# Maxima over partitions of kept attention chunks by VectorE's 32x32 block transposes in place of TensorE's transposes, two more chunks computed twice, and a lower limit on VectorE's shifts

## The chip, the cores and the metric

The kernel runs on one core of one Trainium2 chip. The metric is the device time of one execution in microseconds (us); lower is better. A core has five engines that run side by side, each with its own in-order queue: PE (TensorE, matrix products and transposes), ACT (ScalarE), DVE (VectorE), POOL (GpSimd) and SP (SyncE, which issues all DMAs here). In the profile, PEld is TensorE's load of the stationary operand, which overlaps PE. PE writes to PSUM only; POOL cannot read PSUM. [...]

## The reference, cut to what matters

Two independent layers share the launch, and their outputs are joined along the last axis:

```python
# A: Fourier mixing, S = 2048, D = 448
a = einsum("bsd,ed->bse", x, dft_hid_re);  b = einsum("bsd,ed->bse", x, dft_hid_im)
y = einsum("ts,bse->bte", dft_seq_re, a) - einsum("ts,bse->bte", dft_seq_im, b)
# B: attention, H = 16 heads of Dh = 28
q, k, v = split(x @ wqkv)
p = softmax(einsum("bhqd,bhkd->bhqk", q, k) * Dh**-0.5)
o = concat_heads(einsum("bhqk,bhkd->bhqd", p, v)) @ wo
out = concatenate([y, o], axis=-1)
```

The softmax subtracts each row's maximum over all 2048 keys. The change touches how that maximum is found and applied, for part of the rows.

## The kernel before, in words

**Precision and tiles.** Matrix products run on 32-bit operands split in a high and a low part (three products stand for one). `P = 128`, `CH = 512`, `NT = 16` key tiles, `NC = 4` query chunks of 512 queries for each head. A unit is one (head, chunk) pair; there are 64 of them. Scores are computed transposed, keys on partitions and 512 queries along the free axis, so the maximum over keys goes over 16 tiles and over the 128 partitions of each.

**Two kinds of units.** `TWICE` lists for each head which chunks are computed twice; all others are kept.

- `unit_twice` (lines 743 to 789; 16 units before the change): 16 score products with the queries on partitions (L754), each reduced by DVE along the free axis (L758), one reduction of the 16 results (L762), a small PE transpose (L717), a split in high and low part (L766 on ACT, L767 on DVE), a store of the two rows to DRAM (L770) and their load into two extra rows of the query tile (L771). Then 16 score products again (L782), now with the maximum already subtracted by the extra rows, and 16 exponentials of 512 (L786 on ACT).
- `unit_kept` (lines 791 to 853; 48 units before): 16 score products (L804), each copied from PSUM to SBUF pairs (`kept`, copies at L415, ACT for the most part, DVE for some at L417) and folded by DVE into a running maximum `rm` of 128 x 512 (first L811, then L814). Then the maximum over the 128 partitions: four PE transposes of 128x128 (`turn`, L821), a DVE reduction to 128x4 with the sign changed (L823), four PE transposes of a broadcast operand (`spread`, L830) that leave the negated maximum of each query in all 128 partitions of a PSUM bank `pm`, and an ACT copy of it to `mb` in SBUF (L832). Then each of eight pairs (128x1024) is shifted by it: on POOL with `mb`, or on DVE with `pm` (both L847; DVE may take pairs `i < DVE_SHIFT`, and any pair near the end, `LATE`), and exponentiated on ACT (L851).

Both end in products with the values (`pv_group`, L735) and a copy of the result (`unit_out`); `out_of` (L866 to L884) folds, normalises and stores; the output projection (L976) comes last, with operands split at L958 and L411.

**The fill.** The projections (`project`, `values`), the Fourier layer's first product (`hidden`; all at L547) and its second (`sequence`, L662) are PE work that needs few other engines: weights are loaded (L515), copied to a high part on ACT (L516), and the low part is taken on POOL (L522).

**What sets the order.** Nothing is ordered by hand. `Schedule` (lines 170 to 314) is a planner that runs while the program is built: every task has an engine (or a choice of engines), an assumed cost, a key (a due time) and slots of buffers; it simulates the engines and hands each free engine the ready task with the lowest key, and the program's order on every engine is that. The costs at lines 389 and 390 are its assumptions (`DVE_P = 0.60` for a DVE operation of 512). Kept and twice units form two lanes, with due times spread evenly from `T_ATT` to `T_END` (lines 420 to 429); the fill's keys are spread by `fkey`. At run time the engines meet only through semaphores, and the order does not adapt.

**Buffers at the change.** `rm`, `mb` and `n2` have one slot each, `nm` three; six of eight PSUM banks serve attention (`bank_s`), two the fill.

Of the kernel before, what the change touches and what calls it, by code (L numbers as in the profile page):

```python
# [11 lines left out]
F32 = mybir.dt.float32  # L12
# [10 lines left out]
H = 16  # L23
DH = 28
P = 128
# [5 lines left out]
SCALE = DH ** -0.5  # L31

NKEPT = 19
DVE_SHIFT = 4
LATE = 110.0
NKEYS = 8
NFILL = 2
# [1 line left out]
N_WARM = 11  # L39
GV = 8  # L40

TWICE = [(1,) for h in range(H - 2)] + [(3,), (3,)]
OUT_DVE = True

LAST = (0, 1, 3, 2)
# [2 lines left out]
def f32(ap):  # L48
    return ap.bitcast(F32)
# [268 lines left out]
def tile_kernel(ctx, tc, xa, wre, wim, wd, xb, wqkv, wo, out):  # L318
# [8 lines left out]
    def new(name, shape, dtype=F32, n=None, in_turn=False):  # L327
        if n is None:
            return sb.tile(shape, dtype, tag=name, name=name)
        sch.pools.append(Slots([sb.tile(shape, dtype, tag=f"{name}{i}", name=f"{name}{i}") for i in range(n)], in_turn))  # L330
        return sch.pools[-1]
# [25 lines left out]
    sm_s = new("sm", [P, NT], F32, 1)  # L357
    mx_s = new("mx", [P, 4, NC], F32, 1)
    nm_s = new("nm", [P, 4], F32, 3)
    n2_s = new("n2", [4, 2, P], F32R, 1)  # L360
    banks = [ps.tile([P, CH], F32, tag=f"bank{i}", name=f"bank{i}") for i in range(8)]

    w_first = Weights(lent, held=True)
# [23 lines left out]


    M512, M448, MS = 0.2335, 0.2065, 0.2365
    ACT_P, ACT_S, DVE_P, POOL_2 = 0.48, 0.52, 0.60, 1.25  # L390

    def pe(key, emit, n=1, d=MS, lat=0.25, **kw):
        return sch.add({"PE": n * d}, key, emit, lat=lat, **kw)
# [5 lines left out]
    def act(key, emit, d=ACT_P, **kw):  # L399
        return sch.add({"ACT": d}, key, lambda e: emit(), **kw)  # L400

    def dve(key, emit, d=DVE_P, **kw):
        return sch.add({"DVE": d}, key, lambda e: emit(), **kw)
# [20 lines left out]
    P_R = (T_END - T_ATT) / (len(lane_r) + 1.5)  # L424
    P_K = (T_END - T_ATT) / (len(lane_k) + 1.5)
    due = {}
    for lane, per, ahead, part in ((lane_r, P_R, 1.08, 1.0), (lane_k, P_K, 1.8, 1.0)):
        for i, u in enumerate(lane):
            due[u] = (T_ATT + i * per, T_ATT + (i + ahead) * per, part * per / 16)
    head_due = [min(due[h, c][0] for c in range(NC)) for h in range(H)]  # L430
# [312 lines left out]
    def unit_twice(u):  # L743
        h, c = u
        t_a, t_b, dt = due[u]
        q = q_s.slot()
        lq = load_q(u, q)
        mx, nm = mx_s.slot(), nm_s.slot()
        ms = []
        for kc in range(NC):  # L750
            for qt in range(4):
                o = bank_s.slot()
                key = t_a + (kc * 4 + qt) * dt
                m = pe(key, lambda e, o=o, kc=kc, qt=qt: nc.tensor.matmul(  # L754
                    o.t, q.t[:KR, qt * P:(qt + 1) * P], KT[h][kc].t[:KR, :], start=True, stop=True),
                    deps=[*lq, *got_k[h, kc], before.get("ra")], use=[o, q, KT[h][kc], mx])
                in_line("ra", m)
                ms.append(dve(key - 20, lambda o=o, kc=kc, qt=qt: nc.vector.tensor_reduce(  # L758
                    mx.t[:, qt, kc:kc + 1], o.t, axis=AX.X, op=ALU.max), deps=[m],
                    use=[o, mx]))  # L760
        key = t_a + 16 * dt - 20
        r = dve(key, lambda: nc.vector.tensor_reduce(nm.t, mx.t, axis=AX.X, op=ALU.max, negate=True), 0.2,  # L762
                deps=ms, acq=[nm], use=[mx])
        o, n2 = bank_s.slot(), n2_s.slot()
        t = max_rows(key, o, nm, r)
        a = act(key, lambda o=o: nc.scalar.activation(n2.t[:, 0, :], o.t[:4, :P], AF.Copy), 0.2, deps=[t], acq=[n2], use=[o])  # L766
        b = dve(key, lambda o=o: nc.vector.tensor_tensor(n2.t[:, 1, :], o.t[:4, :P], f32(n2.t[:, 0, :]), op=ALU.subtract), 0.25,  # L767
                deps=[a], use=[o, n2])
        nd = nm_d[h * NC + c]
        s = dma(key, lambda: nc.sync.dma_start(nd.rearrange("r (a b) -> a r b", a=4), f32(n2.t)), size=4, deps=[b], use=[n2])  # L770
        ld = dma(key, lambda: nc.sync.dma_start(f32(q.t)[KR:KR + 2, :], nd), size=4, deps=[s], use=[q])  # L771
        po = bank_s.slot()
        last_pv = None
        for g in range(NT // GV):
            tiles, es = [], []
            for kt in range(GV * g, GV * (g + 1)):
                o = bank_s.slot()
                if kt % 2 == 0:
                    tiles.append(kept_s.slot())
                p = Half(tiles[-1], kt % 2)  # L780
                key = t_b + kt * dt
                m = pe(key, lambda e, o=o, kt=kt: nc.tensor.matmul(  # L782
                    o.t, KT[h][kt // 4].t[:KR + 2, kt % 4 * P:(kt % 4 + 1) * P], q.t[:KR + 2, :], start=True, stop=True),
                    deps=[ld, before.get("rb")], use=[o, p.pair, q, KT[h][kt // 4], po])
                in_line("rb", m)
                es.append(act(key - 20, lambda o=o, p=p: nc.scalar.activation(p.t, o.t, AF.Exp, scale=SCALE),  # L786
                              deps=[m], use=[o, p.pair]))
            last_pv = pv_group(u, g, tiles, [*es, last_pv], po, key)
        unit_out(u, po, last_pv, key - 20)

    def unit_kept(u):
        h, c = u
        t_a, t_b, dt = due[u]
        q = q_s.slot()
        lq = load_q(u, q)
        rm, nm, mb = rm_s.slot(), nm_s.slot(), mb_s.slot()
        kept, cs = [], []
        for kt in range(NT):
            o = bank_s.slot()
            if kt % 2 == 0:  # L800
                kept.append(kept_s.slot())
            s = Half(kept[-1], kt % 2)
            key = t_a + kt * dt
            m = pe(key, lambda e, o=o, kt=kt: nc.tensor.matmul(  # L804
                o.t, KT[h][kt // 4].t[:KR, kt % 4 * P:(kt % 4 + 1) * P], q.t[:KR, :], start=True, stop=True),
                deps=[*lq, *got_k[h, kt // 4], before.get("ka")], use=[o, s.pair, rm, q, KT[h][kt // 4]])
            in_line("ka", m)
            cs.append(sch.add({"ACT": ACT_P, "DVE": DVE_P} if kt == 1 else {"ACT": ACT_P}, key - 20,
                              lambda e, o=o, s=s: copy_of(e, s.t, o.t), deps=[m], use=[o, s.pair], lock=[o]))
            if kt == 1:  # L810
                prev = dve(key - 20, lambda o=o, s=kept[0]: nc.vector.tensor_tensor(rm.t, o.t, s.t[:, 0, :], op=ALU.max),  # L811
                           deps=[m, cs[0]], use=[rm, o, kept[0]], lock=[o], own=RAW)
            elif kt:
                prev = dve(key - 20, lambda o=o: nc.vector.tensor_tensor(rm.t, o.t, rm.t, op=ALU.max),  # L814
                           deps=[m, prev], use=[rm, o], lock=[o], own=RAW)
        key = t_a + 16 * dt - 20
        o = bank_s.slot()

        def turn(e, o=o):
            for i in range(4):  # L820
                nc.tensor.transpose(o.t[:, i * P:(i + 1) * P], rm.t[:, i * P:(i + 1) * P], ident)  # L821
        t = pe(key, turn, d=0.45, deps=[prev], use=[o, rm])
        r = dve(key, lambda o=o: nc.vector.tensor_reduce(  # L823
            nm.t, o.t.rearrange("p (a b) -> p a b", a=4), axis=AX.X, op=ALU.max, negate=True), deps=[t], use=[o, nm])

        pm = bank_s.slot()

        def spread(e):
            for i in range(4):
                nc.tensor.transpose(pm.t[:, i * P:(i + 1) * P], nm.t[:, i:i + 1].to_broadcast([P, P]), ident)  # L830
        t = pe(key, spread, d=0.45, deps=[r], use=[pm, nm])
        ld = act(key, lambda: nc.scalar.activation(mb.t, pm.t, AF.Copy), deps=[t], use=[pm, mb], lock=[pm])  # L832
        po = bank_s.slot()
        last_pv = None
        pairs = NT // 2

        def over_pair(t):
            return bass.AP(tensor=t.tensor, offset=t.offset, ap=[t.ap[0], [0, 2], [1, CH]])

        for g in range(NT // GV):  # L840
            es = []
            for i in range(GV // 2 * g, GV // 2 * (g + 1)):
                s = kept[i]
                key = t_b + 2 * i * dt

                def shift(e, s=s):
                    eng[e].tensor_tensor(s.t, s.t, over_pair(pm.t if e == "DVE" else mb.t), op=ALU.add)  # L847
                on_dve = i < DVE_SHIFT or due[u][0] > T_END - LATE
                sh = sch.add({"POOL": 2.36, "DVE": 1.13} if on_dve else {"POOL": 2.36}, key, shift,
                             deps=[ld, t, cs[2 * i], cs[2 * i + 1]], use=[s, mb, *([pm] if on_dve else [])])  # L850
                es.append(act(key, lambda s=s: nc.scalar.activation(s.t, s.t, AF.Exp, scale=SCALE), 0.96, deps=[sh], use=[s]))  # L851
            last_pv = pv_group(u, g, kept[GV // 2 * g:GV // 2 * (g + 1)], [*es, last_pv], po, key)
        unit_out(u, po, last_pv, key - 20)
# [168 lines left out]
```

## Time and profile before

| what | value |
|---|---|
| median of three runs | 1169.23 us (1166.75 to 1170.17) |
| the profiled execution's own time | 1167.41 us |
| its span from first to last instruction | 1165.6 us |
| mean granted TensorE clock | 0.998 |
| instructions | 19879 |
| DVE reductions at L823, one for each kept unit | 48 |
| DVE reductions at L762, one for each twice unit | 16 |

Busy time is the union of an engine's instructions; an instruction's mean duration can be longer than its turn on the engine, because the next one starts while it ends. In the lists of groups the columns are: line, engine, operation, operands (output, then inputs), shapes, count, then busy us and mean ns of one, then idle time of the engine ahead of them and what ended it. A timeline row begins with start and length in us from the span's start.

### The profile page before, as it was taken

The numbers are of one execution on the slowest core, as the hardware profiler recorded it, in microseconds if no ns is written. First come the engines' busy times: TensorE is split into PE (matmuls) and PEld (weight loads), VectorE is DVE, ScalarE is ACT, GpSimd is POOL, SyncE is SP. The second block draws the span as 40 slices with busy tenths as digits, with TensorE's granted clock in tenths as the row PEclk, the third lists the DMA queues.
The fourth block names the chain that finished last, engine by engine and source line by source line (L and its number), as shares of the span: only waits on it lengthen the run. The fifth ranks groups of instructions, "written<-read, shape, count | busy, mean of one in ns | idle before, by whom it ended". The sixth has DMA issues, their size and how long they took to land.

```text
span 1165.6 us, 19879 instructions
## 1 busy us (share of the span) xinstructions
PE 1155.8 (99%) x6426; PEld 810.0 (69%) x6426; DVE 934.8 (80%) x1473; ACT 1054.0 (90%) x1773; POOL 908.1 (78%) x530
## 2 busy tenths in 40 slices
PE   8999999999999999999999999999999999999998
PEld 7876666676766766766766676767767666667687
DVE  6699978888878878887888889888888878878742
ACT  5279999999999999999999999999999999999942
POOL 2167768999888889888978998998887898996830
PEclk9999999999999999999999999999999999999999
DMA  8892345231323242322223332323224333223552
GB/s 257 178 212 105 120 126 179 75 92 58 95 79 105 70 117 70 99 78 90 87 89 91 94 113 71 99 74 107 90 80 117 90 102 94 86 70 88 181 166 105
DMA packets 111736, 125.18 MB, mean 107 GB/s; under 512 B 49264, under 2 KB 63216, under 8 KB 111632
## 3 DMA queue, kind: packets, MB, share of 16 engines
q1 hardware_dynamic: 111632, 123.91, 36.0%
q8 instruction: 51, 0.84, 0.3%
q14 instruction: 53, 0.43, 0.1%
HBM read 89.98 MB, written 33.75 MB: 106 GB/s over the span
## 4 chain that ended last, share of the span: by engine, by line
PE 94%; DVE 2%; POOL 1%; issue 1%; ACT 1%; DMA 1%; SPq 0%; DVEq 0%; ACTq 0%
PE bank L662 27%; PE bank L735 19%; PE bank L804 15%; PE bank L547 13%; PE bank L782 5%; PE bank L754 5%; PE bank L976 3%; PE bank L821 2%; PE bank L830 2%; PE bank L866 1%; DVE rm L814 1%; POOL kept L847 1%; DMA kept<-wqkv 0%; DVE big L411 0%; ACT kept L415 0%
## 5 line engine op out<-in xcount | busy, mean ns | idle before, releaser
L847 POOL TENSOR_TENSOR kept<-kept,mb 128x1024 f32<-128x1024 f32 x262 | 626.0, 2412 | 111.1 <-ACT mb L832 87.3
L814 DVE TENSOR_TENSOR rm<-bank,rm 128x512 f32<-128x512 f32 x672 | 460.4, 685 | 74.9 <-ACT kept L415 27.3
L415 ACT ACTIVATE kept<-bank 128x512 f32<-128x512 f32 (+1 forms) x711 | 410.2, 634 | 55.7 <-PE bank L804 31.9
L851 ACT ACTIVATE kept<-kept 128x1024 f32<-128x1024 f32 x371 | 394.2, 1103 | 9.1 <-POOL kept L847 7.4
L662 PE MATMUL bank<-big,whi 128*128 128x448 f32 x1024 | 324.5, 369 | 0.0
L804 PE MATMUL bank<-q,k 84*128 84x512 f32 x768 | 290.2, 408 | 0.2
L522 POOL TENSOR_TENSOR wlo<-wraw,whi 128x512 fp32r<-128x512 f32 (+1 forms) x166 | 205.0, 1239 | 95.2 <-ACT whi L516 61.7
L735 PE MATMUL bank<-kept,v 128*32 128x512 f32 x1984 | 241.6, 600 | 0.0
L662 PEld LDWEIGHTS bank<-big,whi 128*128 128x128 f32 x1024 | 193.2, 189 | 31.5 <-issue 6.2
L662 PE MATMUL bank<-big,wlo 128*128 128x448 f32 x512 | 188.3, 368 | 0.0
L804 PEld LDWEIGHTS bank<-q,k 84*128 84x128 f32 x768 | 141.8, 189 | 63.7 <-DVE rm L814 14.7
L758 DVE TENSOR_REDUCE mx<-bank 128x1 f32<-128x512 f32 x256 | 173.9, 681 | 12.4 <-PE bank L754 11.6
L786 ACT ACTIVATE kept<-bank 128x512 f32<-128x512 f32 x250 | 159.6, 643 | 3.6 <-PE bank L782 3.4
L735 PEld LDWEIGHTS bank<-kept,v 128*32 128x32 f32 x1984 | 56.1, 109 | 124.1 <-issue 115.0
L847 DVE TENSOR_TENSOR kept<-kept,bank 128x1024 f32<-128x1024 f32 x109 | 131.5, 1210 | 0.2
L516 ACT ACTIVATE whi<-wraw 128x512 fp32r<-128x512 f32 x167 | 113.7, 681 | 12.9 <-DMA wraw<-wqkv 10.7
L662 PEld LDWEIGHTS bank<-big,wlo 128*128 128x128 f32 x512 | 96.8, 189 | 12.8
L754 PE MATMUL bank<-k,q 84*128 84x512 f32 x256 | 104.7, 410 | 0.0
L782 PE MATMUL bank<-q,k 86*128 86x512 f32 x256 | 104.2, 410 | 0.2 <-DVE rm L814 0.2
L547 PE MATMUL bank<-wd,whi 128*128 128x448 f32 x256 | 80.1, 368 | 0.0
L547 PE MATMUL bank<-big,whi 128*128 128x512 f32 x196 | 70.0, 400 | 1.4 <-DVE big L411 1.1
L823 DVE TENSOR_REDUCE nm<-bank 128x4 f32<-128x512 f32 x48 | 33.1, 690 | 46.3 <-PE bank L821 42.1
(81 smaller groups left out, 1064.5 us busy)
## 6 DMA issues: line engine op xcount, KB each, us to landing
wraw<-wre SPq DMA_DIRECT2D x64, 256.0 KB
wraw<-wim SPq DMA_DIRECT2D x64, 256.0 KB
qkd<-wd SPq DMA_DIRECT2D x32, 256.0 KB
wraw<-xa SPq DMA_DIRECT2D x32, 256.0 KB
k<-qkd SPq DMA_DIRECT2D x64, 112.0 KB
q<-qkd SPq DMA_DIRECT2D x64, 112.0 KB
out<-kept SPq DMA_DIRECT2D x30, 224.0 KB
qkd<-kept SPq DMA_DIRECT2D x24, 256.0 KB
```

The source lines that it names most:

```text
L415: nc.scalar.activation(dst, src, AF.Copy)
L522: b = sch.add(e, at, lambda g: eng[g].tensor_tensor(self.lo.t[:, :n], raw.t[:, :n], f32(self.hi.t)[:, :n], op=ALU.subtract), deps=[a], acq ...
L547: nc.tensor.matmul(o.t[:, :cols], w(), x(), start=(i == 0), stop=(i == n - 1))
L662: nc.tensor.matmul(o.t[:, :D], a.t[:, k, :], b[:, q * 4 + k, :], start=(q == 0 and k == 0 and j == 0), stop=(q == 3 and k == 3 and j == 2))
L735: nc.tensor.matmul(o.t[j * VW:(j + 1) * VW, :], VT[h].t[:, kt // 4, j, :], pairs[i // 2].t[:, i % 2, :], start=(kt < 4), stop=(kt >= NT - 4))
L754: m = pe(key, lambda e, o=o, kc=kc, qt=qt: nc.tensor.matmul(o.t, q.t[:KR, qt * P:(qt + 1) * P], KT[h][kc].t[:KR, :], start=True, stop=True ...
L758: ms.append(dve(key - 20, lambda o=o, kc=kc, qt=qt: nc.vector.tensor_reduce(mx.t[:, qt, kc:kc + 1], o.t, axis=AX.X, op=ALU.max), deps=[m], ...
L782: m = pe(key, lambda e, o=o, kt=kt: nc.tensor.matmul(o.t, KT[h][kt // 4].t[:KR + 2, kt % 4 * P:(kt % 4 + 1) * P], q.t[:KR + 2, :], start=T ...
L804: m = pe(key, lambda e, o=o, kt=kt: nc.tensor.matmul(o.t, KT[h][kt // 4].t[:KR, kt % 4 * P:(kt % 4 + 1) * P], q.t[:KR, :], start=True, sto ...
L814: prev = dve(key - 20, lambda o=o: nc.vector.tensor_tensor(rm.t, o.t, rm.t, op=ALU.max), deps=[m, prev], use=[rm, o], lock=[o], own=RAW)
L847: eng[e].tensor_tensor(s.t, s.t, over_pair(pm.t if e == "DVE" else mb.t), op=ALU.add)
L851: es.append(act(key, lambda s=s: nc.scalar.activation(s.t, s.t, AF.Exp, scale=SCALE), 0.96, deps=[sh], use=[s]))
```

## The change

It has five parts. In `unit_kept` the eight PE transposes go. DVE transposes `rm` in blocks of 32x32 into a PSUM bank, reduces it (512 to 16 elements on each partition, negated), copies three blocks of 32 partitions beside the first (three copies of 32x16), reduces these four (32x4x16 to 32x16), copies the result to the other partitions (32x16, then 64x16), and transposes it in blocks of 32x32, read with a broadcast, into the bank `pm`. Two more chunks, chunk 3 of heads 4 and 10, become twice units: 18 twice, 46 kept. `DVE_SHIFT` goes from 4 to 3. The second half of a kept unit is due at 1.9 periods in place of 1.8. In `unit_twice` the small tile `n2` is laid out over partitions (high part at 0, low part at 32) and stored by two DMAs in place of one.

```diff
-DVE_SHIFT = 4
+DVE_SHIFT = 3
-TWICE = [(1,) for h in range(H - 2)] + [(3,), (3,)]
+TWICE = [(1, 3) if h in (4, 10) else (1,) for h in range(H - 2)] + [(3,), (3,)]
...
-    n2_s = new("n2", [4, 2, P], F32R, 1)
+    n2_s = new("n2", [64, P], F32R, 1)
+    m_s = new("m", [P, 5, NT], F32, 1)
...
-    for lane, per, ahead, part in ((lane_r, P_R, 1.08, 1.0), (lane_k, P_K, 1.8, 1.0)):
+    for lane, per, ahead, part in ((lane_r, P_R, 1.08, 1.0), (lane_k, P_K, 1.9, 1.0)):
...
+        def put():
+            for i in range(2):
+                nc.sync.dma_start(nd[i:i + 1].rearrange("r (a b) -> (r a) b", a=4), f32(n2.t[32 * i:32 * i + 4]))
+        s = dma(key, put, size=2, n=2, deps=[b], use=[n2])
...
-        def turn(e, o=o):
-            for i in range(4):
-                nc.tensor.transpose(o.t[:, i * P:(i + 1) * P], rm.t[:, i * P:(i + 1) * P], ident)
-        t = pe(key, turn, d=0.45, deps=[prev], use=[o, rm])
+        t = dve(key, lambda o=o: nc.vector.transpose(o.t, rm.t), deps=[prev], acq=[o], use=[rm])
+        mq = m_s.slot()
         r = dve(key, lambda o=o: nc.vector.tensor_reduce(
-            nm.t, o.t.rearrange("p (a b) -> p a b", a=4), axis=AX.X, op=ALU.max, negate=True), deps=[t], use=[o, nm])
+            mq.t[:, 0], o.t.rearrange("p (j r) -> p j r", r=32), axis=AX.X, op=ALU.max, negate=True), deps=[t], use=[o, mq], own=RAW)
+        def beside(i):
+            return lambda: nc.vector.tensor_copy(mq.t[:32, i], mq.t[32 * i:32 * i + 32, 0])
+        def back(n):
+            return lambda: nc.vector.tensor_copy(mq.t[n:2 * n, 4], mq.t[:n, 4])
+        r = [dve(key, beside(i), SMALL, deps=[r], use=[mq], own=RAW) for i in (1, 2, 3)]
+        r = dve(key, lambda: nc.vector.tensor_reduce(
+            mq.t[:32, 4], mq.t[:32, :4].rearrange("p i j -> p j i"), axis=AX.X, op=ALU.min), 0.13, deps=r, use=[mq], own=RAW)
+        for n in (32, 64):
+            r = dve(key, back(n), SMALL, deps=[r], use=[mq], own=RAW)
-        def spread(e):
-            for i in range(4):
-                nc.tensor.transpose(pm.t[:, i * P:(i + 1) * P], nm.t[:, i:i + 1].to_broadcast([P, P]), ident)
-        t = pe(key, spread, d=0.45, deps=[r], use=[pm, nm])
+        t = dve(key, lambda: nc.vector.transpose(pm.t, bass.AP(
+            tensor=mq.t.tensor, offset=mq.t.offset + 4 * NT, ap=[mq.t.ap[0], [1, NT], [0, 32]])), deps=[r], use=[pm, mq], own=RAW)
         ld = act(key, lambda: nc.scalar.activation(mb.t, pm.t, AF.Copy), deps=[t], use=[pm, mb], lock=[pm])
```

More of the change, by code (lines that the diff above doesn't have):

```diff
@@ L389, in tile_kernel @@
     M512, M448, MS = 0.2335, 0.2065, 0.2365
-    ACT_P, ACT_S, DVE_P, POOL_2 = 0.48, 0.52, 0.60, 1.25
+    ACT_P, ACT_S, DVE_P, POOL_2, SMALL = 0.48, 0.52, 0.60, 1.25, 0.1
     def pe(key, emit, n=1, d=MS, lat=0.25, **kw):
@@ L765, in unit_twice @@
         t = max_rows(key, o, nm, r)
-        a = act(key, lambda o=o: nc.scalar.activation(n2.t[:, 0, :], o.t[:4, :P], AF.Copy), 0.2, deps=[t], acq=[n2], use=[o])
-        b = dve(key, lambda o=o: nc.vector.tensor_tensor(n2.t[:, 1, :], o.t[:4, :P], f32(n2.t[:, 0, :]), op=ALU.subtract), 0.25,
+        a = act(key, lambda o=o: nc.scalar.activation(n2.t[:4], o.t[:4, :P], AF.Copy), 0.2, deps=[t], acq=[n2], use=[o])
+        b = dve(key, lambda o=o: nc.vector.tensor_tensor(n2.t[32:36], o.t[:4, :P], f32(n2.t[:4]), op=ALU.subtract), 0.25,
                 deps=[a], use=[o, n2])
         nd = nm_d[h * NC + c]
-        s = dma(key, lambda: nc.sync.dma_start(nd.rearrange("r (a b) -> a r b", a=4), f32(n2.t)), size=4, deps=[b], use=[n2])
+        def put():
+            for i in range(2):
+                nc.sync.dma_start(nd[i:i + 1].rearrange("r (a b) -> (r a) b", a=4), f32(n2.t[32 * i:32 * i + 4]))
+        s = dma(key, put, size=2, n=2, deps=[b], use=[n2])
         ld = dma(key, lambda: nc.sync.dma_start(f32(q.t)[KR:KR + 2, :], nd), size=4, deps=[s], use=[q])
@@ L795, in unit_kept @@
         lq = load_q(u, q)
-        rm, nm, mb = rm_s.slot(), nm_s.slot(), mb_s.slot()
+        rm, mb = rm_s.slot(), mb_s.slot()
         kept, cs = [], []
```

## Prediction, written before the result

> **What bounds the kernel now.** I read the page's busy line first, then the chain of work that ended last by line, then the busy times by stretch.
>
> ```profile
> span 1165.6 us, 19879 instructions
> PE 1155.8 (99%) x6426; PEld 810.0 (69%) x6426; DVE 934.8 (80%) x1473; ACT 1054.0 (90%) x1773; POOL 908.1 (78%) x530
> ...
> by line: PE bank L662 27.1%; PE bank L735 19.5%; PE bank L804 15.5%; PE bank L547 12.7%; PE bank L782 5.3%; PE bank L754 5.2%; PE bank L976 3.1%; PE bank L821 2.1%; PE bank L830 1.8%; PE bank L866 1.5%; DVE rm L814 1.3%; issue 0.9%; POOL ke
> ...
> 100.00:1085.00 985.00, 982.69 (x5570) 670.95 (x5569) 826.77 (x1264) 954.68 (x1600) 841.80 (x475) 1.00 0.31 94
> ```
>
> The last row gives, for the stretch from 100 to 1085 us, busy PE, PEld, DVE, ACT, POOL, then clock and DMA. PE is full (983 of 985) and the chain is nearly all PE, so time taken off PE counts. But ACT stands close behind at 97% of that stretch, POOL at 85% and DVE at 84%: what is taken off PE may be met by the next engine. The chain ends with a tail, which tells how much PE is worth there:
>
> ```profile
> 1110.72 1.85 PE bank L735 x16
> 1112.58 2.44 PE bank L976 x11
> 1130.63 1.28 POOL L880 TENSOR_TENSOR kept<-kept 64x512 f32<-64x512 f32 x1 [0.91 <-DMA kept<-rd]
> 1153.23 9.01 PE bank L976 x44
> ```
>
> The first row is the last product with values, ended at 1112.6; the span ends 53 us later. The last output projections (9.0 us) need the last normalisation (POOL, L880, ended at 1131.9). If nothing else were in the way, that normalisation's store and load, the split, 9 us of products and the last store would put the end near 1150 by my estimate, some 38 us behind the last attention product. The other 15 us are fill of L662 that PE had left over. So the end is the later of two things: all of PE's work, or attention's end plus 38 us.
>
> **What PE is rid of.** Four transposes take PE this long, from one PEld start to the next of another line:
>
> ```profile
> 546.04 0.51 PEld L821 LDWEIGHTS bank<-ident,rm 128*128 128x128 f32 x4
> 546.52 0.19 PEld L754 LDWEIGHTS bank<-k,q 84*128 84x128 f32 x1
> ...
> 547.75 0.56 PEld L830 LDWEIGHTS bank<-ident,nm 128*128 128x128 f32 x4
> 548.28 0.19 PEld L804 LDWEIGHTS bank<-q,k 84*128 84x128 f32 x1
> ```
>
> That is 0.48 and 0.53 us. The chain says the same: 2.1% + 1.8% of 1165.6 is 45.5 us over 96 groups, 0.47 us each. All 96 go (46 kept units have none, two units are kept no more): **-45.5 us**.
>
> Two more twice units add 2 x 16 score products. A kept unit has 16 (L804), a twice unit 32 (L754, L782); by the chain L804 takes 15.5% of 1165.6 over 768, 0.235 us each: 32 x 0.235 = **+7.5 us**. Their two small transposes (L717) add 2 x 0.27 = 0.5 us at most. Products with values and the fill stay. PE's work falls by 37.5 us; with nothing else changed the profiled execution's 1167.4 us become **1129.9**. That is the floor while PE keeps its present waits.
>
> **What DVE takes on.** Rows of groups (count, then busy us and mean ns):
>
> ```profile
> L814 DVE TENSOR_TENSOR rm<-bank,rm 128x512 f32<-128x512 f32 x672 | 460.4, 685 | 74.9 <-ACT kept L415 27.3 <-PE bank L804 23.6 <-ACT mb L832 0.5
> L758 DVE TENSOR_REDUCE mx<-bank 128x1 f32<-128x512 f32 x256 | 173.9, 681 | 12.4 <-PE bank L754 11.6
> L847 DVE TENSOR_TENSOR kept<-kept,bank 128x1024 f32<-128x1024 f32 x109 | 131.5, 1210 | 0.2
> L823 DVE TENSOR_REDUCE nm<-bank 128x4 f32<-128x512 f32 x48 | 33.1, 690 | 46.3 <-PE bank L821 42.1 <-ACT kept L851 3.6 <-ACT kept L786 0.3
> L417 DVE COPY ou<-bank 128x512 f32<-128x512 f32 x42 | 28.8, 686 | 9.6 <-PE bank L735 8.8
> L767 DVE TENSOR_TENSOR n<-bank,n 4x128 fp32r<-4x128 f32 x16 | 4.3, 272 | 2.3 <-ACT n L766 2.2
> L762 DVE TENSOR_REDUCE nm<-mx 128x4 f32<-128x16 f32 x16 | 2.6, 162 | 0.1
> L616 DVE MEMSET kept<- 128x16 f32 x16 | 1.2, 72 | 0.0
> ```
>
> No block transpose is in the trace. Nearest is a copy of the same 128x512 (L417, 0.69 us); the far end is twice the work at one port, a 128x1024 operation (L847, 1.21 us). I take 0.69. The Trainium skill ("Vector Engine (DVE) Microarchitecture Reference", 3.8 The reshape front-end and per-opcode configuration) says that the block transpose sustains one element per cycle per lane; by its slope and fixed cost (5.2) I estimate 0.61 us, which would make the sum 7 us smaller, and no run here shows it yet.
>
> The five copies of 16 elements lie between 0.07 (L616) and 0.27 us (L767): I take 0.10, as they are nearest to L616 in size. The second reduction is like L762, 0.16 (up to 0.27). The big reduction stays at 0.69, with more outputs. One unit's addition: 2 x 0.69 + 5 x 0.10 + 0.16 = **2.04 us** (bounds 1.8 and 4.04). Times 46: 94 us.
>
> The rest of DVE: a kept unit's maxima take 460.4/48 + 0.68 + 0.69 = 11.0 us, a twice unit's 173.9/16 + 0.16 + 0.27 = 11.3; two units changed, +0.6. DVE shifted 109 pairs, 2.3 a unit, so a limit of 3 bites seldom: I take 100 for 46 units, -9 x 1.21 = -11 us. In the stretch (43 units of 45) DVE's 826.8 become 826.8 + 87.7 + 0.6 - 10 = **905 us**. Against that a wait goes: DVE stood 42.1 us in front of L823 for PE's transposes, since its queue is in order. It disappears, as all eight steps are now on DVE itself.
>
> **What the others get.** A kept unit costs ACT the copies, the exponentials and `mb`, a twice unit 16 exponentials of 512:
>
> ```profile
> L415 ACT ACTIVATE kept<-bank 128x512 f32<-128x512 f32 x701 | 404.8, 635 | 33.4 <-PE bank L804 31.9 <-DVE rm L814 0.2
> L851 ACT ACTIVATE kept<-kept 128x1024 f32<-128x1024 f32 x371 | 394.2, 1103 | 9.1 <-POOL kept L847 7.4 <-DVE kept L847 1.3
> L786 ACT ACTIVATE kept<-bank 128x512 f32<-128x512 f32 x250 | 159.6, 643 | 3.6 <-PE bank L782 3.4
> L832 ACT ACTIVATE mb<-bank 128x512 f32<-128x512 f32 x48 | 30.1, 627 | 3.4 <-PE bank L830 1.5 <-ACT kept L415 0.9 <-issue 0.8
> L847 POOL TENSOR_TENSOR kept<-kept,mb 128x1024 f32<-128x1024 f32 x262 | 626.0, 2412 | 111.1 <-ACT mb L832 87.3 <-PE bank L804 8.5 <-ACT kept L415 5.1
> ```
>
> That is (404.8 + 394.2 + 30.1)/48 = 17.3 us against 159.6/16 + 0.3 = 10.3: two units make **-14 us**, so ACT's 954.7 of the stretch become 941. POOL: 16 pairs fewer to shift in all, some 9 of them DVE's, so 7 x 2.41 = -17 us. Both get lighter, and this hides nothing.
>
> The split store of `n2` makes 18 x 2 - 16 = 20 more DMAs, each one turn of SP's queue:
>
> ```profile
> L770 SPq DMA_DIRECT2D nmd<-n x16: 253/274/463, 99.7 to 1030.1; - x16
> ```
>
> So 20 x 0.27 = 5.5 us of SP in 1165, 0.27 us for each twice unit ahead of L771 and of whatever load stands behind it on SP. A twice unit has over 50 us of its lane's period to hide it in; without that cover, 18 x 0.27 = 5 us. I cost it at nothing, and the due time of 1.9 too: it changes which ready task is taken first, not the work (uncovered: later shifts leave POOL idle, which the POOL row above bounds at another 87 us of waits).
>
> **The chain of one unit.** From the last maximum to `mb` the trace has two PE groups, one reduction and the ACT copy: the unit of the rows above starts L821 at 546.04 and has `mb` at 549.2, 3.2 us. Now eight dependent DVE steps come first: 2.04 + 0.69 = 2.7 us of work, some 0.1 of hand-over at each, and `mb` 0.6: 4 us if nothing gets between, up to 8 if the planner puts another 0.6 us operation into each gap. Behind these steps on DVE stand the next unit's maxima (L811, L814), whose banks PE needs; for `mb` wait POOL's and DVE's shifts, then the exponentials. POOL idles already 87.3 us for `mb`, 33 times; one to four us more per unit fits in POOL's idle 143 us of the stretch only in part, so this is what gives back some of the gain.
>
> **Sum.** Attention's end: DVE at 95% of a stretch needs 905/0.95 = 953 us, ACT at 98% needs 941/0.98 = 960; 985 shrinks by some 25. Attention would end at 1088, plus 38 is 1126: PE's floor of 1129.9 is later and bounds. To it I add 10 us, by choice: PE's waits for the running maximum are 1.3% of the chain (15 us), and DVE's idle time in the stretch falls from 158 to some 50 us, so these waits grow by perhaps two thirds. **1140 us** for the profiled execution; its own 1167.4 lies 1.8 under the median, within the spread of the three runs, so I leave it at 1140.
>
> **Rivals.**
>
> *DVE becomes the bound.* With the addition at 3.5 us a unit (steps with gaps that nothing fills, slow transposes), DVE's stretch is 905 + 43 x 1.46 = 968 us, at 97% 998: attention ends 13 us later, 1125.6 + 38 = 1164. At the upper price of 4.04, 991/0.98 = 1012 gives 1178. For it: all engines above 90%, in a fixed order. Against: the 42 us of freed wait, and that at 2.04 it does not bind. Its time: 1150 to 1178, middle 1164.
>
> *The copies wait for POOL (slower).* The trace has a DVE operation with both inputs in SBUF, L411, beside a running POOL operation:
>
> ```profile
> L411 DVE TENSOR_TENSOR k<-kept,k x32: 412/423/1524, 1096.9 to 1153.8; 128x256 fp32r<-128x256 f32 x24, 64x256 fp32r<-64x256 f32 x8
> ...
> 1106.31 2.72 POOL L522 TENSOR_TENSOR wlo<-wraw,whi 128x512 fp32r<-128x512 f32 x2
> ...
> 1106.96 0.92 DVE L411 TENSOR_TENSOR k<-kept,k 128x256 fp32r<-128x256 f32 x1 [1.09 <-ACT k L958]
> ...
> 1107.91 1.41 DVE L411 TENSOR_TENSOR k<-kept,k 64x256 fp32r<-64x256 f32 x1
> ```
>
> Alone it takes 0.42 us. Here the first ends some 0.2 us behind the first POOL operation (at about 1107.67), the second 0.28 us behind the second (1109.03): each DVE operation of this kind lets one whole POOL operation go by. If the five copies, SBUF to SBUF, do the same, a unit can lose up to 5 x 2.41 = 12 us of DVE (1590 us in all, the far end). One whole POOL shift a unit, 2.41, makes DVE's stretch 905 + 104 = 1009, at 98% 1030: attention's end 1157, plus 38: **1195 us**. It decides from 1.7 us a unit: 905 + 73 = 978, at 98% 998, hence 1164. Against it: in 33 of 48 units POOL already stood idle for `mb`, that is, in the very time in which the copies run, and it cannot start a shift of the new unit before they are done. The Trainium skill ("SBUF — State Buffer", Who interferes with whom) has this as its rule: copies with source and destination in SBUF may use a second port that DVE and POOL lock against each other for a whole instruction, and reductions do not. By that rule this rival holds whenever POOL is busy at the copies; the L411 rows agree on two-input operations, and no row shows a copy.
>
> *PE's time is not released.* If the transposes sat in time that PE would have waited anyway, nothing is saved and 7.5 are added: 1167 to 1175. Against it: the chain has 3.9% on them, and PE's next products start right behind.
>
> **Chances.** Forecast, 1128 to 1150, likeliest 1140: 0.58. DVE the bound: 0.20. Copies wait for POOL: 0.16. PE's time not released: 0.06. What a measurement can tell from no change is about 0.3%, 3.5 us. Faster: 0.58 and 0.15 of the second; same: 0.05 of the second and 0.03 of the last; slower: 0.16 and 0.03. Range: 1124 (2 us under the attention bound) to 1175 (nearly all of the second and all of the last), which leaves out the POOL case and little else, about 0.18.
>
> **What would show it.** Right: no L821 or L830, block transposes near 0.69 us, copies near 0.1, DVE busy above 88% of the span, PE still 98%. Wrong: copies with means above 0.5 us whose long ones end with a POOL operation; DVE above 95%, with PE or ACT waiting for the running maximum; block transposes above 1 us; POOL's wait for `mb` grown well past 87 us; or PE idle in the stretch by more than 20 us.

## The result: slower, 1281.3 us against 1169.7

The changed kernel takes 1281.32 us (median of four, 1276.11 to 1283.44), the kernel before 1169.7 us in the same comparison: a ratio of 1.0946, 95% interval 1.09 to 1.0992. The forecast was 1140 with a range up to 1175. The chain by engine before:

```profile
PE 94%; DVE 2%; POOL 1%; issue 1%; ACT 1%; DMA 1%; SPq 0%; DVEq 0%; ACTq 0%
```

The profile after, page lines first, then the chain by engine, then the stretch from 100 to 1085 us with the columns as in the prediction (length, then busy PE, PEld, DVE, ACT, POOL, clock, DMA, GB/s):

```profile
span 1278.8 us, 19407 instructions
PE 1185.7 (93%) x6076; PEld 796.3 (62%) x6076; DVE 1110.1 (87%) x1819; ACT 1051.8 (82%) x1761; POOL 923.5 (72%) x536
...
PE 46%; DVE 33%; ACT 11%; issue 6%; DMA 2%; POOL 1%; SPq 0%; DVEq 0%; ACTq 0%; POOLq 0%
...
100.00:1085.00 985.00, 906.11 (x4677) 593.88 (x4679) 891.61 (x1429) 852.72 (x1420) 783.76 (x438) 0.96 0.27 84
```

Before, the chain was 94% PE; now DVE has a third of it. Every engine does less per us than before (PE 906 of 985 where it was 983, ACT 853 where it was 955) except DVE, at 892. DVE's groups at the change:

```profile
L831 DVE COPY m<-m 32x16 f32<-32x16 f32 x138 | 93.4, 677 | 2.6
L842 DVE STREAM_TRANSPOSE bank<-m 128x512 f32<-128x512 f32 x46 | 33.2, 723 | 1.3
L824 DVE STREAM_TRANSPOSE bank<-rm 128x512 f32<-128x512 f32 x46 | 33.1, 719 | 1.0
...
L834 DVE COPY m<-m 64x16 f32<-64x16 f32 x46 | 16.7, 363 | 1.5
L834 DVE COPY m<-m 32x16 f32<-32x16 f32 x46 | 15.8, 343 | 1.5
L836 DVE TENSOR_REDUCE m<-m 32x16 f32<-32x64 f32 x46 | 11.5, 249 | 1.4
```

The block transposes take 0.72 us, near what was assumed. The copies of 16 elements do not: 677 ns on average. The answer for their line tells more, as it gives minimum, median and maximum in ns:

```profile
L831 DVE COPY m<-m x138: 161/167/4654, 68.7 to 1209.6; 32x16 f32<-32x16 f32 x138
```

Most take 0.17 us and some take up to 4.65. A mean four times the median points to a wait that is counted as busy time. What such a copy waits for is seen when DVE's and POOL's timelines are laid side by side at a long one:

```profile
415.85 5.73 DVE L831 COPY m<-m 32x16 f32<-32x16 f32 x3
421.61 0.25 DVE L836 TENSOR_REDUCE m<-m 32x16 f32<-32x64 f32 x1
```

```profile
415.59 1.28 POOL L523 TENSOR_TENSOR wlo<-wraw,whi 128x512 fp32r<-128x512 f32 x1 [0.85 <-ACT whi L517]
416.84 4.71 POOL L859 TENSOR_TENSOR kept<-kept,mb 128x1024 f32<-128x1024 f32 x2
```

Three copies begin at 415.85 while POOL runs, and end at 421.58, when POOL's second shift ends (421.55). Three copies let three POOL operations go by. The whole trace says the same: of the 230 small copies 81 took over 0.25 us, and each of these began while a POOL operation ran and ended 23 to 36 ns after the end of a POOL operation, 73 at the first such end and 8 at a later one. No copy ran from start to end within a POOL operation. That is the second rival of the prediction. PE waits for DVE in turn:

```profile
PEld bank L809 <- DVE rm L816: 44.0, 24, 4.8
PE bank L809 <- DVE rm L816: 33.9, 17, 4.4
```

These are the waits of the score products for the first running maximum, 78 us in all. Before, PE waited there (L804 for L811) for 0.3 us. The tail is nearly as long as before; three rows of the chain's end:

```profile
1226.59 1.85 PE bank L736 x16
...
1254.65 2.23 PE bank L663 x11
...
1266.11 9.10 PE bank L988 x44
```

From the last product with values (ended 1228.4) to the end of the span are 50.4 us; before, 53.0.

### The profile page after: what moved, and what is told of

Read it like the earlier page. It is cut to its first block, busy times and chain, and to the rows that moved or that the text cites. A ratio compares the mean times of both kernels' runs of the same rounds, so it can differ in the third digit from the quotient of the medians.

```text
span 1278.8 us, 19407 instructions
## 1 busy us (share of the span) xinstructions
PE 1185.7 (93%) x6076; PEld 796.3 (62%) x6076; DVE 1110.1 (87%) x1819; ACT 1051.8 (82%) x1761; POOL 923.5 (72%) x536
## 4 chain that ended last, share of the span: by engine, by line
PE 46%; DVE 33%; ACT 11%; issue 6%; DMA 2%; POOL 1%; SPq 0%; DVEq 0%; ACTq 0%; POOLq 0%
PE bank L663 13%; DVE rm L819 10%; PE bank L736 9%; PE bank L809 8%; PE bank L548 7%; DVE m L831 7%; ACT kept L416 5%; PE bank L988 3%; PE bank L755 3%; DVE mx L759 3%; PE bank L787 3%; ACT kept L863 2%; DVE bank L824 2%; ACT kept L791 2%; DVE m L826 2%
## 5 line engine op out<-in xcount | busy, mean ns | idle before, releaser
L859 POOL TENSOR_TENSOR kept<-kept,mb 128x1024 f32<-128x1024 f32 x270 | 642.6, 2402 | 130.1 <-ACT mb L844 113.2
L819 DVE TENSOR_TENSOR rm<-bank,rm 128x512 f32<-128x512 f32 x644 | 440.8, 684 | 67.4 <-ACT kept L416 29.7
L416 ACT ACTIVATE kept<-bank 128x512 f32<-128x512 f32 (+1 forms) x684 | 388.5, 615 | 103.9 <-PE bank L809 76.5
L863 ACT ACTIVATE kept<-kept 128x1024 f32<-128x1024 f32 x353 | 372.0, 1084 | 8.5 <-POOL kept L859 6.1
L663 PE MATMUL bank<-big,whi 128*128 128x448 f32 x1024 | 333.1, 377 | 0.0
L663 PEld LDWEIGHTS bank<-big,whi 128*128 128x128 f32 x1024 | 199.6, 195 | 30.2 <-issue 3.5
L759 DVE TENSOR_REDUCE mx<-bank 128x1 f32<-128x512 f32 x288 | 195.5, 682 | 11.4 <-PE bank L755 10.0
L663 PE MATMUL bank<-big,wlo 128*128 128x448 f32 x512 | 192.6, 376 | 0.0
L787 PE MATMUL bank<-q,k 86*128 86x512 f32 x288 | 119.0, 419 | 10.6 <-DVE rm L816 4.4
L755 PE MATMUL bank<-k,q 84*128 84x512 f32 x288 | 118.6, 417 | 8.0 <-DVE rm L816 6.1
L663 PEld LDWEIGHTS bank<-big,wlo 128*128 128x128 f32 x512 | 100.0, 195 | 16.6 <-issue 3.4
L859 DVE TENSOR_TENSOR kept<-kept,bank 128x1024 f32<-128x1024 f32 x83 | 99.8, 1210 | 1.2 <-ACT mb L844 0.9
L831 DVE COPY m<-m 32x16 f32<-32x16 f32 x138 | 93.4, 677 | 2.6
L787 PEld LDWEIGHTS bank<-q,k 86*128 86x128 f32 x288 | 55.2, 192 | 47.2 <-DVE rm L819 9.3
```

The source lines that it names most:

```text
L416: nc.scalar.activation(dst, src, AF.Copy)
L663: nc.tensor.matmul(o.t[:, :D], a.t[:, k, :], b[:, q * 4 + k, :], start=(q == 0 and k == 0 and j == 0), stop=(q == 3 and k == 3 and j == 2))
L787: m = pe(key, lambda e, o=o, kt=kt: nc.tensor.matmul(o.t, KT[h][kt // 4].t[:KR + 2, kt % 4 * P:(kt % 4 + 1) * P], q.t[:KR + 2, :], start=T ...
L831: return lambda: nc.vector.tensor_copy(mq.t[:32, i], mq.t[32 * i:32 * i + 32, 0])
```

## The experiments

Theory 1: the five copies from SBUF to SBUF wait for POOL's running operation, and these waits are the loss. Theory 2: the chain of eight dependent DVE steps and the planned order are the loss, whatever the copies cost. Ratios are to the kernel before in the same comparison, with a 95% interval.

**Copies written as reductions.** Same values, same order on every engine; only the operation of five steps differs.

```diff
-            return lambda: nc.vector.tensor_copy(mq.t[:32, i], mq.t[32 * i:32 * i + 32, 0])
+            return lambda: nc.vector.tensor_reduce(mq.t[:32, i], mq.t[32 * i:32 * i + 32, 0].rearrange("p (j o) -> p j o", o=1), axis=AX.X, op=ALU.max)
-            return lambda: nc.vector.tensor_copy(mq.t[n:2 * n, 4], mq.t[:n, 4])
+            return lambda: nc.vector.tensor_reduce(mq.t[n:2 * n, 4], mq.t[:n, 4].rearrange("p (j o) -> p j o", o=1), axis=AX.X, op=ALU.max)
```

> The changed kernel with its five small copies (L831, L834) written as reductions over one element, which give the same values; the order of every engine stays as in the changed kernel. Theory 1 (the copies wait for POOL's running operation, and that is the loss): the five steps fall from 2.7 us a unit to below 1.0, DVE's busy time falls by 80 us or more, and the time comes to 1140 to 1170. Theory 2 (the chain of eight dependent steps on DVE and the planner's order around it are the loss, whatever the copies cost): 1220 or more, with PE still waiting for the first running maximum (L816) by some 80 us.

1178.73 us, ratio 1.0088 (1.0057 to 1.0119): 103 us come back by the kind of five instructions. The busy line, the stretch and the two lines' durations:

```profile
PE 1149.4 (98%) x6076; PEld 772.0 (66%) x6076; DVE 1020.2 (87%) x1819; ACT 1044.5 (89%) x1761; POOL 923.0 (78%) x536
...
100.00:1085.00 985.00, 968.93 (x5205) 631.96 (x5204) 896.23 (x1578) 937.78 (x1574) 860.14 (x479) 0.99 0.29 93
...
L831 DVE TENSOR_REDUCE m<-m x138: 156/158/163, 71.0 to 1107.6; 32x16 f32<-32x16 f32 x138
...
L834 DVE TENSOR_REDUCE m<-m x92: 158/161/165, 73.0 to 1108.2; 32x16 f32<-32x16 f32 x46, 64x16 f32<-64x16 f32 x46
```

No step lasts over 0.17 us any more, though 160 of the 230 ran wholly within a POOL operation, and DVE has 90 us less busy time. Theory 1 holds for the size of the loss. But 1179 is above the 1140 to 1170 it expected: without any wait for POOL, the change still gains nothing. That is a second question.

**Spare copies and spare reductions in the kernel before**, five of 32x16 behind each L823, results unused:

```diff
+        spare = m_s.slot()
+        for i in range(5):
+            dve(key, lambda i=i: nc.vector.tensor_copy(spare.t[:32, i], zeros[:32]), 0.1, deps=[r], use=[nm, spare])
```

> The kernel before, with five spare copies of 32x16 from SBUF to SBUF on DVE behind each L823, whose results nobody uses (and n2 laid out as in the changed kernel). Theory 1: the copies wait for POOL as in the changed kernel, their mean is 0.4 us or more, some last over 2 us, and the kernel slows to 1190 to 1260. Theory 2: copies at 0.17 us, 1167 to 1180.

> As the run with spare copies, but with five spare reductions of 32x16x1 in their place. Both theories: 0.17 to 0.2 us each, none above 0.4, 1167 to 1185. Its distance from the run with copies is the price of waiting alone.

1197.85 us (1.0254, 1.0217 to 1.0292) with copies, 1175.2 (1.0054, 1.003 to 1.0079) with reductions. Their durations, first the copies, then the reductions:

```profile
L835 DVE COPY m<-zeros x240: 98/155/8717, 71.7 to 1125.8; 32x16 f32<-32x16 f32 x120
```

```profile
L835 DVE TENSOR_REDUCE m<-zeros x240: 99/147/150, 69.7 to 1101.3; 32x16 f32<-32x16 f32 x120
```

In the other kernel, with PE's transposes in place, copies of 16 elements cost 23 us more than reductions of 16, with single ones up to 8.7 us. The copies' mean was 0.275 us, below the expected 0.4. POOL was at work when the reduction ahead of them ended in 22 of 48 units, against 38 of 46 in the changed kernel.

**The planner told of the copies' mean price** (`SMALL` 0.55 in place of 0.1).

> The changed kernel, with the planner told that each small copy takes 0.55 us (about the measured mean) in place of 0.1. Theory 1: the waits are real DVE time that no plan removes: 1230 to 1300. If the loss comes from the order being planned with wrong costs: below 1210.

1294.73 us (1.1084, 1.1044 to 1.1123). Knowing the mean does not help: a copy takes 0.17 us or waits, by what POOL runs at that moment.

**All parts of the change but the block transposes** (18 twice, limit 3, 1.9, `n2`).

> The kernel before with every part of the change but the block transposes: 18 chunks twice, a limit of 3 on DVE's shifts, 1.9 in place of 1.8, n2 over partitions. PE's transposes stay. PE gets 8 us more work and bounds: 1170 to 1182. If the other parts themselves upset the plan: above 1190.

1180.11 us (1.0091, 1.0071 to 1.0111). With PE's transposes in place, the other parts cost 12 us, somewhat over the 8 us of PE work that they add.

**True prices.** Reductions for copies, and `SMALL` 0.16, the small reduction 0.25, the block transposes 0.64.

> The changed kernel with reductions for copies, and the planner told the measured turns: 0.16 for a small step, 0.25 for the small reduction, 0.64 for a block transpose. If what is left of the loss is DVE's load and the chain, hardly a change: 1165 to 1185. If it is an order planned with wrong prices: below 1160.

1164.84 us (0.9964, 0.995 to 0.9977): 14 us under the run with the old prices, and the only version with the full maximum that beats both kernels, the one before by 0.4%. Both expectations had a part of it: the prices, and so the order, matter, and most of the expected gain stays away. Against the run with all other parts, true prices gain 15 us: that is what the transposes' move is worth here, and the other parts take 12 of it back. No run has the move without them.

**The chain short, and the load gone.** In both, the second transpose reads the first reduction's result; in one the six small steps follow later, in the other they are left out.

```diff
-            tensor=mq.t.tensor, offset=mq.t.offset + 4 * NT, ap=[mq.t.ap[0], [1, NT], [0, 32]])), deps=[r], use=[pm, mq], own=RAW)
+            tensor=mq.t.tensor, offset=mq.t.offset, ap=[mq.t.ap[0], [1, NT], [0, 32]])), deps=[r0], use=[pm, mq], own=RAW)
```

> The changed kernel with reductions for copies; the second block transpose reads the result of the first reduction, so the maximum is that of a quarter of the partitions, and the six small steps are done later, for nobody. DVE's load is the same, the chain to mb is about 2 us shorter. If DVE's load is what keeps the gain away: 1165 to 1180. If the chain's length is: 1140 to 1155.

> As the run with the steps aside, but the six small steps are left out altogether (the maximum is that of a quarter of the partitions): DVE has 46 x 1.05 = 48 us less. If DVE's load keeps the gain away: 1140 to 1155, clearly below the run with the steps aside. If the chain's length does: the same as that run.

1185.81 us (1.0144, 1.011 to 1.0178) aside, 1155.76 (0.9887, 0.9861 to 0.9913) gone; each lies a little above the range expected for it if DVE's load decides. A shorter chain alone gains nothing (it is 7 us slower than the run with reductions, and its order differs); less DVE work does. The two share the short chain, and 30 us lie between them for some 48 us of DVE; beside the run with reductions it is 23 us.

**More twice units, and fewer shifts on DVE**, both on top of true prices.

> The run with true prices, and four more chunks computed twice (chunk 3 of heads 2, 6, 8 and 12: 22 twice, 42 kept). PE gets 4 x 3.75 = 15 us more, ACT some 28 us less, POOL some 50 us less, DVE some 20 us less. If the other engines' load is what is left of the loss: 1140 to 1160. If PE bounds: 1175 to 1185.

> The run with true prices, and DVE may shift two pairs of a unit at most: POOL takes some 30 pairs more (72 us), DVE some 36 us less. If DVE's load alone is left: 1145 to 1160. If POOL has no room for them, or ACT bounds: 1165 to 1185.

1185.69 us (1.0133, 1.0112 to 1.0153) and 1182.54 (1.0101, 1.006 to 1.0143). Relieving DVE by loading another engine loses: with two shifts POOL is busy for 927 of the stretch's 985 us. The run with 22 twice units lost 21 us against true prices, more than the 15 us of PE work; why is not settled. DVE, ACT and POOL all had more room in it (first row; the second is the run with two shifts), so DVE's load alone does not hold the end of the version with true prices.

```profile
100.00:1085.00 985.00, 977.40 (x5296) 647.00 (x5296) 862.70 (x1522) 916.52 (x1557) 807.23 (x460) 0.99 0.30 94
...
100.00:1085.00 985.00, 972.83 (x5235) 636.57 (x5234) 866.78 (x1550) 936.34 (x1572) 927.16 (x508) 0.99 0.29 93
```

**What is PE's time worth?** In the kernel before, one transpose of four in each group; then the same with three spare DVE reductions of 128x512 behind L823.

```diff
-            for i in range(4):
-                nc.tensor.transpose(o.t[:, i * P:(i + 1) * P], rm.t[:, i * P:(i + 1) * P], ident)
+            nc.tensor.transpose(o.t[:, :P], rm.t[:, :P], ident)
...
-            for i in range(4):
-                nc.tensor.transpose(pm.t[:, i * P:(i + 1) * P], nm.t[:, i:i + 1].to_broadcast([P, P]), ident)
+            nc.tensor.transpose(pm.t[:, :P], nm.t[:, :1].to_broadcast([P, P]), ident)
```

> The kernel before with one of four transposes in each of the two PE groups (the reduction and the bank pm read that one block four times, so three quarters of the queries get another query's value as their maximum); DVE, ACT and POOL do as much as before. PE has 96 x 0.47 x 3/4 = 34 us less. If PE's time on the transposes bounds, as the prediction has it: 1130 to 1142. If ACT or the plan hold the end where it is: 1155 or more.

> As the run with a quarter of the transposes, and three spare reductions of 128x512 on DVE behind each L823, 2.1 us a unit, for nobody (and n2 over partitions): the DVE load of the changed kernel without its chain, and with nothing that waits for POOL. If DVE's load alone takes the gain back: 1155 to 1175. If it needs the chain of dependent steps: below 1148.

1166.01 us (0.9977, 0.9961 to 0.9994): of 34 us of PE work, 2 came through. With the spare load 1181.77 (1.0105, 1.0078 to 1.0131), 16 us more. So DVE's load costs, and the first step of the prediction, that PE's time comes off the end, is wrong already in the kernel before. Its stretch, without the load:

```profile
100.00:1085.00 985.00, 976.90 (x5337) 647.66 (x5336) 835.10 (x1279) 954.66 (x1605) 852.24 (x481) 0.99 0.30 95
```

ACT is busy 954.66 us, to a tenth what it was before (954.68). Hence the last question, whether ACT bounds beside PE:

**ACT relieved**, with a quarter of the transposes, with all, and in the version with true prices:

```diff
-                es.append(act(key, lambda s=s: nc.scalar.activation(s.t, s.t, AF.Exp, scale=SCALE), 0.96, deps=[sh], use=[s]))
+                es.append(act(key, lambda s=s: nc.scalar.activation(s.t[:, :, :384], s.t[:, :, :384], AF.Exp, scale=SCALE), 0.75, deps=[sh], use=[s]))
```

> The run with a quarter of the transposes, and the exponentials of kept pairs taken over 384 of each 512 columns only (the rest stays unexponentiated), the planner told 0.75 us: ACT has some 384 x 0.21 = 80 us less. If ACT, at 97% of the stretch, is what held the end at 1166 although PE had 34 us less: 1125 to 1145. If it is the order or something else: 1155 or more.

> The kernel before, with the same cut of ACT's exponentials and all PE transposes in place. If PE bounds by itself before: 1158 to 1170, nothing gained. If ACT alone bounded before: 1145 or less. Beside the run with both cut it tells whether the two engines bind together, so that neither cut alone pays.

> The changed kernel with reductions for copies and true prices, and the same cut of ACT's exponentials. If ACT is the next engine there too: 1130 to 1148. If DVE, at 91% of the stretch with its chain, holds the end: 1155 to 1165, as without the cut.

| PE's transposes | ACT as before | ACT relieved |
|---|---|---|
| all (kernel before) | 1169.7 | 1171.05, ratio 1.0001 (0.9987 to 1.0015) |
| a quarter | 1166.01, ratio 0.9977 (0.9961 to 0.9994) | 1142.33, ratio 0.9758 (0.9739 to 0.9778) |
| none, on DVE (true prices) | 1164.84, ratio 0.9964 (0.995 to 0.9977) | 1166.6, ratio 0.996 (0.9942 to 0.9978) |

Neither cut pays alone, both together give 28 us: PE and ACT bound together before. (The planner was told of each cut, so the order differs too; no run holds it fixed.) In the last row ACT's relief gives nothing: there something else holds the end. The stretches of the run with both cuts, and of true prices with ACT relieved, this one with its chain by engine:

```profile
100.00:1085.00 985.00, 982.69 (x5452) 656.90 (x5451) 842.01 (x1290) 908.98 (x1650) 853.62 (x483) 1.00 0.33 99
```

```profile
100.00:1085.00 985.00, 976.89 (x5289) 638.79 (x5288) 892.42 (x1571) 899.37 (x1625) 877.56 (x493) 1.00 0.31 95
...
PE 88%; DVE 5%; ACT 3%; DMA 2%; issue 1%; POOL 1%; SPq 0%; ACTq 0%; DVEq 0%; POOLq 0%
```

With both cut, PE is full again and ACT has room (909). In the second, ACT has room too, and DVE stands at 892, where the kernel before had 827. That DVE has taken ACT's place there is likely but not shown: the chain is 88% PE and 5% DVE, and no run relieves DVE and ACT together.

## Why the prediction was wrong, point by point

- **The copies at 0.10 us, and the POOL rival at 0.16.** This is the step that failed by the most. Without a wait a small step takes 0.16 us; with it L831 averages 0.677 and L834 0.353. Over 138 and 92 instructions that is 138 x 0.519 + 92 x 0.192 = 89 us of DVE, 1.9 us a unit on top of what the steps cost by themselves, and swapping the kind of instruction gave 103 us back. The L411 rows had shown the wait for operations of two inputs, and the rule of the Trainium skill ("SBUF — State Buffer", Who interferes with whom) covered copies; the run with reductions agrees with both halves of it, copies held and reductions not. What outweighed them was a false argument: that POOL stands idle for `mb` when the copies run. In the kernel before it did so in 33 of 48 units, for 1.6 us in the median, just ahead of `mb`, at the end of the chain. The copies come earlier: in the changed kernel POOL was still at work, with the fill or the previous unit's shifts, when they began in 38 of 46 units. The rival's sum (1195) was low too, though its wait of 2.41 us a unit was above the measured 1.9: it let DVE be busy for 98% of the stretch before attention's end moves, where the profile after has DVE at 91% and the last product with values ended at 1228 in place of the rival's 1157.
- **PE's -37.5 us as the floor.** The groups' cost was right, the conclusion was not. A chain that is 94% PE was read as "time taken off PE counts". The run with a quarter of the transposes gained 2 us for 34. ACT, read correctly at 97% of the stretch, was treated as a limit with slack left (941/0.98), though only the cut of both engines' work together brought the end forward.
- **The end as attention plus 38 us.** From the last product with values to the end of the span it took 53.0 us before and 50.4 after. The fill left over in it (10, 7, 5, 1, 11 and 6 products in the same order, as the L662 and L663 rows of the chain show) is placed there by the plan, and did not move forward into the time that PE had free.
- **DVE's addition of 2.04 us.** The transposes were right (0.72 for 0.69; the estimate of 0.61 was further off), the small steps too cheap: 2 x 0.72 + 5 x 0.16 + 0.25 = 2.5 us without waits. The first rival's 1150 to 1178 holds the run with true prices (1165), and the run with old prices (1179) lies just above, but that is luck in part: the rival took 3.5 us a unit and DVE at 97% of the stretch, and here it is 2.5 us and 900 of 985 us, 91%. DVE's load costs; that DVE alone binds is not shown. The 14 us between the two are the order planned with 0.1 for 0.16 and 0.13 for 0.25.
- **The limit of 3 on DVE's shifts.** It was assumed to leave 100 of 109 pairs on DVE. It left 88 (83, and 5 on lent tiles) of 111 (109, and 2 on lent tiles, which the prediction left out).
- **Right:** PE's transposes do go, the block transposes are near a copy's price, and the second DMA of `n2` shows in one wait of PE, of 1.5 us.

What stays open: how much of the last 25 us between 1165 and the forecast is DVE's load and how much the order. Load is shown to cost (six steps gone: -23 us; spare reductions: +16), but lowering it at POOL's or PE's expense lost. The order is shown to count as well, as new prices for the same steps gave 14 us, but no run tells what a better one would give.

## What to carry to other kernels

When four engines are above 80% of a stretch and two above 95%, as here, do not count time taken off one of them as a gain: cut it alone in an experiment and see what comes through, before you move the work to a third. A small copy between SBUF tiles on VectorE beside a busy GpSimd can cost the rest of a GpSimd operation or more, not only its own length: here 0.55 us on average, up to 4.65. The same move as a reduction over one element cost 0.16 us and never waited. A median far under the mean in a group of equal instructions is the sign to look for.

## What the runs showed of the hardware that was not expected

- A VectorE copy of 32x16 from SBUF to SBUF took 0.17 us by itself and up to 4.65 us (8.7 in the kernel before with spare copies) while GpSimd ran; that is more than one GpSimd shift of 2.4 us, so a copy did not always get in at the first end of a GpSimd operation. Written as a reduction over one element, the same move took 0.17 us at most.
- PE's granted clock was lower where PE waited more: in the stretch 0.96 after the change, with PE busy 906 of 985 us, and 1.00 before, with 983; over the whole run 0.965, and 0.996 once the copies no longer waited. That the waits lower the clock is read from these pairs alone. A product at L663 took 377 ns on average, where the same product had taken 369 before (L662, second row):

```profile
L663 PE MATMUL bank<-big,whi 128*128 128x448 f32 x1024 | 333.1, 377 | 0.0
...
L662 PE MATMUL bank<-big,whi 128*128 128x448 f32 x1024 | 324.5, 369 | 0.0
```
